# Streaming 32 columns in the narrow matmuls at the end of a cached-attention decode kernel, with a bias moved and two fills dropped

## The chip, the cores and the metric

The kernel runs on one NeuronCore of one Trainium2 chip. The metric is the device time of one execution, in microseconds (us). A profiled execution leaves a page and a trace; the span of a trace, from its first to its last instruction, is about 1.7 us shorter than the device time of the same execution. One execution of the kernel before, at 1652.69 us, was slow and is left out everywhere, from the medians too.

Names: PE is TensorE (its matmuls), PEld its weight loads, DVE is VectorE, ACT is ScalarE, SP is SyncE. L495 is line 495 of the kernel's file. Line numbers below L600 are almost the same in all versions; behind it they shift by a few lines, so each fence is introduced in words.

## The reference

One decode step for 8 sequences of one token: layer norm with modulation, grouped-query attention over a cache of 8192 positions (8 key/value heads, 32 query heads, 128 wide), the output projection, then a second layer norm and a two-layer MLP with squared ReLU.

```
h   = layernorm(x) * (1 + ca) + sa
q   = h @ wq                                   # 8 x 4096
p   = softmax(q k^T / sqrt(128))               # per head over 8192 positions
x   = x + ga * (concat(p v) @ wo)
h   = layernorm(x) * (1 + cb) + sb
x   = x + gb * (relu(h @ w1 + b1)**2 @ w2 + b2)
```

The caches are 268 MB in bf16, and they are read once.

## The kernel before

Keys and values come in tiles of 4 MB through a ring of four slots: for each of the 8 sequences four key tiles and four value tiles, each holding two heads. What matters here is the end: the value tiles of the last sequence, the output projection, the second norm and the MLP. `op` records an instruction for an engine with the tokens it waits for.

```python
def pe_stream(n, at):                       # "fills": results are never read
    rhs = IDENT[:, :].unsqueeze(1).to_broadcast([128, 4, 128])
    for _ in range(n):
        op("tensor", lambda e: e.matmul(bank(at)..., IDENT[:, :], rhs))          # 512 columns

wide = lambda ap, n=8: ap.unsqueeze(1).to_broadcast([128, n, B])                 # repeats the 8 columns n times
attn_w = bank(4)[:, 0:64 * KT].rearrange("p (k a b) -> p k a b", k=KT, a=8)

def project(q0, q1, k_oP):                  # output projection of the first heads, early
    ...
    op("tensor", lambda e: e.matmul(attn_w[:, k, :, :], wo_sb[...], wide(oP[:, j, g, :]), ...), [k_oP, d_woe])

# last sequence, value tiles p = 0, 1, 2
for m in range(32): ...                     # P @ V, 512 columns, four side by side in the array
t = op("vector", ... tensor_copy(osb, Obank))       # the copy: PE waits for it
...                                         # 4 small matmuls, a DVE multiply
if lastb and p == 1:
    k_oP = early(0, 2, ...)                 # 16 small matmuls and a DVE copy
    for f in range(FT): op("tensor", ... b1 into hT_ps ...)        # bias of the first MLP layer, 14 matmuls
    project(0, 2, k_oP)                     # first call, 64 matmuls
if lastb and p == 2:
    ...
    project(2, 3, k_oP)                     # second call, 32 matmuls

# last value tile (p = 3) arrives in four parts
for m in range(24):
    if m == 16:
        pe_stream(5, 7)
    ...                                     # parts 0 and 1
pe_stream(2, 7); direct(96, 112, ...)       # part 2, 32 columns
...; pe_stream(2, 7); direct(112, 128, ...) # part 3, 32 columns
...                                         # last projection, norm, first MLP layer (W1)
for f in range(FT):                         # second MLP layer (W2), 28 matmuls
    if f in (8, F2):
        pe_stream(1, 7)
    ...
```

The full listing follows.

## Time and profile before

| kernel before | value |
|---|---|
| time, the first three runs | 671.17 us median (671.04 to 671.33) |
| span of the trace | 669.8 us |
| DMA, HBM read | 423 GB/s, DMA busy nine tenths busy or more in all but the last slice |
| PE busy | 498.4 us (74%) |

The page's slices of the span (DMA busy in tenths), and its summary of the chain of work that ended last:

```profile
DMA  9999999999999999999999999999999999999996
PE 53%; DMA 37%; DVE 6%; ACT 2%; issue 1%; SPq 0%
```

Over most of the span DMA sets the pace. The next fence is the chain of waits of the kernel before in order of time: start, length, what. "PE PS L495 x64" is a run of 64 matmuls of line 495.

```profile
561.66 26.55 DMA ring<-in_A_k_cache_dram
...
644.88 3.25 PE PS L495 x64
648.13 2.13 PE PS L580 x32
...
652.25 1.15 PE PS L495 x32
653.40 0.98 PE PS L641 x16
654.38 1.19 PE PS L438 x5
655.57 0.55 PE PS L641 x8
...
658.05 0.20 DVE oTn L656
...
662.21 1.76 PE PS L699 x49
...
664.51 1.04 PE PS L716 x16
665.55 0.32 PE PS L438
665.88 0.53 PE PS L716 x8
666.41 0.32 PE PS L438
666.73 0.33 PE PS L716 x4
```

To be seen: after 588 us the chain never meets DMA again. L495 is the early projection (its first call takes 3.25 us, its second, half as many matmuls, 1.15 us), L580 the third value tile, L641 parts of the fourth, L438 the fills, L699 the first MLP layer, L716 the second with its two fills. A count can fall short of the matmuls issued, since the chain leaves some records out.

The trace also records when transfers land. The data are there before PE wants them (for parts 2 and 3 the first use is the weight load, elsewhere the first matmul):

```
                          landing us   first use by PE us
third value tile             646.5          648.06
fourth tile, part 0          651.4          653.3
fourth tile, part 1          653.9          655.5
fourth tile, part 2          655.2          656.3
fourth tile, part 3          656.5          657.2
W2, last part                665.3          666.66
```

So PE is about 0.75 us behind the last value part and 1.3 us behind the last weights. By this trace that is all there is to gain at this place.

The last view is the busy time of each engine in stretches of 3.41 us; the column after POOL is the granted TensorE clock as a share of full speed, then the DMA share and GB/s.

```profile
core 0: us, PE busy (x) PEld busy (x) DVE busy (x) ACT busy (x) POOL busy (x), PEclk, DMA share, GB/s
645.21:648.63 3.42, 3.42 (x65) 3.06 (x65) 0.00 (x0) 0.00 (x0) 0.00 (x0) 0.50 0.95 402
648.63:652.04 3.41, 2.32 (x54) 0.96 (x42) 0.95 (x3) 0.00 (x0) 0.00 (x0) 1.00 0.99 404
652.04:655.45 3.41, 3.23 (x55) 1.77 (x53) 0.15 (x1) 0.00 (x0) 0.00 (x0) 1.00 1.01 402
...
658.87:662.28 3.41, 2.75 (x34) 1.21 (x31) 1.65 (x9) 0.90 (x3) 0.00 (x0) 1.00 0.94 375
662.28:665.69 3.41, 3.07 (x73) 2.52 (x73) 0.78 (x4) 0.00 (x0) 0.00 (x0) 1.00 0.26 100
```

Each record of the clock but the last, which ends with the trace, lasts 3.413 us or a whole multiple of it (6.827, 20.48, 51.2), at 0.50 or 1.00; the stretches are cut at these borders. From 645.2 to 648.6 us PE had half its clock, and the early projection lies in just that stretch: its matmuls start 53 ns apart there, 31 ns apart in the second call. After 648.6 us the clock was full until the matmuls were over.

### The profile page before, as it was taken

To read this page: it belongs to the slowest core of one execution; us is meant where nothing else is said; L and a number is where in the kernel's file an instruction comes from. 1 tells how busy PE (TensorE), PEld (TensorE's weight loads), DVE (VectorE), ACT (ScalarE), POOL (GpSimd) and SP (SyncE) were. 2 spreads that over 40 slices of the span, in tenths; PEclk is the share of its full clock that TensorE was granted. 3 is DMA by queue.
4 is the path that set the end of the run, shared out by engine and by line. 5 is a ranking of instruction groups with operands and counts; after the bars stand their busy time and mean duration, and the time that the engine had idled before them with its cause. 6 is when DMAs were issued, how large, how long until landed. Compare 5 with 4: busy or idle time off the path is not lost.

```text
span 669.8 us, 16142 instructions
## 1 busy us (share of the span) xinstructions
PE 498.4 (74%) x7467; PEld 342.5 (51%) x7467; DVE 299.3 (45%) x568; ACT 235.1 (35%) x281; POOL 17.0 (3%) x67
## 2 busy tenths in 40 slices
PE   2295964799639993699648995399836996489977
PEld 2274731676218751477316762287415773177644
DVE  2153731466306661367315672166513673156722
ACT  2052620366105650266204660056402662046600
POOL 7200000000000000000000000000000000000000
PEclk9997996799958996699967998699966999579989
DMA  9999999999999999999999999999999999999996
GB/s 375 431 403 430 425 430 434 433 427 432 434 432 434 423 434 434 432 432 425 434 434 432 429 427 433 436 436 423 430 434 436 433 427 427 434 436 436 427 410 237
DMA packets 12970, 283.96 MB, mean 424 GB/s; under 512 B 1266, under 2 KB 2323, under 8 KB 4372
## 3 DMA queue, kind: packets, MB, share of 16 engines
q1 hardware_dynamic: 12900, 283.65, 98.9%
q8 instruction: 13, 0.21, 0.1%
q14 instruction: 9, 0.07, 0.0%
q10 hardware_dynamic: 48, 0.02, 0.0%
HBM read 283.66 MB, written 0.01 MB: 423 GB/s over the span
## 4 chain that ended last, share of the span: by engine, by line
PE 53%; DMA 37%; DVE 6%; ACT 2%; issue 1%; SPq 0%
DMA ring<-in_A_k_cache_dram 37%; PE PS L447 36%; PE PS L462 9%; DVE Pm L552 3%; PE PS L580 3%; ACT KTb L452 1%; PE PS L438 1%; ACT P_sb L530 1%; DVE m L467 1%; PE PS L539 1%; PE PS L495 1%; PE PS L559 0%; DVE O_sb L589 0%; DVE rhs_r L556 0%; DVE Dm L521 0%
## 5 line engine op out<-in xcount | busy, mean ns | idle before, releaser
L452 ACT ACTIVATE KTb<-PS 128x1024 bf16<-128x1024 bf16 x192 | 196.5, 1024 | 377.3 <-PE PS L447 377.3
L447 PE MATMUL PS<-IDENT,ring 128*128 128x128 bf16 x4096 | 267.4, 227 | 51.4 <-DMA ring<-in_A_k_cache_dram 42.7
L447 PEld LDWEIGHTS PS<-IDENT,ring 128*128 128x128 bf16 x4096 | 246.9, 102 | 99.7 <-DMA ring<-in_A_k_cache_dram 43.8
L454 DVE COPY KTb<-PS 128x1024 bf16<-128x1024 bf16 x320 | 209.8, 687 | 150.7 <-PE PS L447 148.5
L580 PE MATMUL PS<-ring,Pm 128*32 128x512 bf16 x992 | 81.4, 486 | 64.0 <-DMA ring<-in_A_v_cache_dram 63.1
L589 DVE CAST O_sb<-PS 128x512 bf16<-128x512 f32 x31 | 21.4, 691 | 145.0 <-PE PS L580 145.0
L462 PE MATMUL PS<-KTb,Qb 128*32 128x512 bf16 x1024 | 78.8, 384 | 4.5 <-ACT KTb L452 4.5
L580 PEld LDWEIGHTS PS<-ring,Pm 128*32 128x32 bf16 x992 | 29.1, 114 | 101.0 <-DMA ring<-in_A_v_cache_dram 64.4
L438 PE MATMUL PS<-IDENT 128*128 128x512 bf16 x137 | 36.3, 380 | 0.0
L593 PEld LDWEIGHTS PS<-SEL,O_sb 128*128 128x128 bf16 x124 | 5.3, 99 | 45.5 <-DVE O_sb L589 45.5
L530 ACT ACTIVATE P_sb<-PS,negm 128x512 bf16<-128x512 f32 x32 | 21.5, 685 | 18.9 <-DVE negm L526 18.9
L593 PE MATMUL PS<-SEL,O_sb 128*128 128x8 bf16 x124 | 8.0, 170 | 24.8 <-DVE O_sb L589 24.8
L462 PEld LDWEIGHTS PS<-KTb,Qb 128*32 128x32 bf16 x1024 | 15.4, 94 | 21.0 <-ACT KTb L452 8.5
L552 DVE COPY Pm<-PS 64x512 bf16<-64x512 bf16 x48 | 19.5, 419 | 13.4 <-PE PS L539 12.4
L467 DVE TENSOR_REDUCE m<-PS 128x1 f32<-128x512 f32 x32 | 22.0, 689 | 6.6 <-PE PS L462 6.6
L539 PE MATMUL PS<-IDENT,P_sb 128*64 128x128 bf16 x512 | 20.4, 222 | 2.0 <-ACT P_sb L530 1.2
L539 PEld LDWEIGHTS PS<-IDENT,P_sb 128*64 128x64 bf16 x512 | 15.2, 109 | 9.8 <-ACT P_sb L530 9.8
L438 PEld LDWEIGHTS PS<-IDENT 128*128 128x128 bf16 x137 | 11.3, 103 | 12.7 <-issue 4.7
L596 DVE TENSOR_TENSOR oTn<-PS,rinv 128x8 bf16<-128x8 f32 x31 | 6.0, 193 | 11.0 <-PE PS L593 11.0
L549 ACT ACTIVATE Pm<-PS 64x512 bf16<-64x512 bf16 x16 | 9.5, 592 | 1.1
L398 PE MATMUL PS<-haT,ring 128*128 128x8 bf16 x128 | 3.6, 168 | 7.5 <-DMA ring<-in_A_wq_dram 7.5
L689 ACT ACTIVATE std<-PS,epst 128x8 f32<-128x8 f32 x1 | 0.3, 267 | 23.3 <-PE PS L687 23.3
(114 smaller groups left out, 100.8 us busy)
## 6 DMA issues: line engine op xcount, KB each, us to landing
ring<-in_A_k_cache_dram SPq DMA_DIRECT2D x32, 4096.0 KB, 35.1
ring<-in_A_v_cache_dram SPq DMA_DIRECT2D x31, 4096.0 KB, 28.0
ring<-in_A_wq_dram SPq DMA_DIRECT2D x1, 4096.0 KB, 20.7
ring<-in_w_mod_dram SPq DMA_DIRECT2D x1, 3072.0 KB, 10.3
wo_sb<-in_A_wo_dram SPq DMA_DIRECT2D x1, 3072.0 KB, 45.6
ring<-in_A_v_cache_dram SPq DMA_DIRECT2D x1, 2048.0 KB, 22.5
ring<-in_B_w_dram SPq DMA_DIRECT2D x3, 512.0 KB, 17.6
ring<-in_B_w_dram SPq DMA_DIRECT2D x1, 1344.0 KB, 20.0
```

The costliest lines, as they stand in the source:

```text
L438: op("tensor", lambda e: e.matmul(bank(at).rearrange("p (a r) -> p a r", a=4), IDENT[:, :], rhs))
L447: t = op("tensor", lambda e, j=j, i=i: e.matmul(STG[j][:, i, :], src[:, 32 * k + 8 * j + i, :], IDENT[:, :], is_transpose=True), [loaded[n ...
L452: stg_free[j] = op("scalar", lambda e, j=j, dst=dst: e.activation(dst, STG[j], ACT.Copy), [t], "scaP")
L454: stg_free[j] = op("vector", lambda e, j=j, dst=dst: e.tensor_copy(dst, STG[j]), [t], "vecP")
L462: t = op("tensor", lambda e, hf=hf, q=q, rhs=rhs: e.matmul(PS[32 * q:32 * (q + 1), k, :], Qb[:, 2 * p + hf, :], rhs, start=(p == 0 and hf ...
L467: return op("vector", lambda e: e.tensor_reduce(m4[:, k:k + 1], bank(k), AX.X, ALU.max), [t])
L530: exps.append(op("scalar", lambda e, k=k: e.activation(P_sb[:, k, :], bank(k), ACT.Exp, bias=negm[:, 0:1], scale=inv_sqrt, accum_out=rs4[: ...
L539: t = op("tensor", lambda e, k=k, i=i, hf=hf, src=src: e.matmul(STG[k][64 * hf:64 * (hf + 1), i, :], src, IDENT[:, :], is_transpose=True, ...
L552: done.append(op("vector", lambda e, dst=dst, frm=frm: e.tensor_copy(dst, frm), [t, k_pm], "vecP"))
L580: t = op("tensor", lambda e, p=p, m=m, cg=cg, vt=vt, Obank=Obank: e.matmul(Obank[32 * cg:32 * (cg + 1), :], lhs[:, p, 32 * m:32 * m + 32], ...
L589: t = op("vector", lambda e, osb=osb, Obank=Obank: e.tensor_copy(osb, Obank), [t], "vecP")
L593: t = op("tensor", lambda e, i=i, osb=osb, oT_ps=oT_ps: e.matmul(oT_ps, osb[:, i * 128:(i + 1) * 128], SEL[:, i, :], start=(i == 0), stop= ...
```

## The change

The intent: make the early projection stream 32 columns instead of 64, since in the trace of before the 32-column matmuls of the fourth tile start 25 ns apart at full clock, and the 64-column ones of the projection 31 ns apart, 53 ns at half clock; put the bias matmuls where fills had been; drop the fills of the second MLP layer. The diff, with lines cut that only follow from it:

```diff
-        wide = lambda ap, n=8: ap.unsqueeze(1).to_broadcast([128, n, B])
-        attn_w = bank(4)[:, 0:64 * KT].rearrange("p (k a b) -> p k a b", k=KT, a=8)
+        wide = lambda ap: ap.unsqueeze(1).to_broadcast([128, 4, B])
+        attn_w = bank(4)[:, 0:32 * KT].rearrange("p (k a b) -> p k a b", k=KT, a=4)
...                                  (hT_w and oT_w likewise: PSUM spacing only)
                     if lastb and p == 1:
                         k_oP = early(0, 2, [norm_last, k_all] + stg_free + hold)
-                        for f in range(FT):
-                            op("tensor", ... b1 into hT_ps ...)
                         project(0, 2, k_oP)
...
                         if m == 16:
-                            pe_stream(5, 7)
+                            pe_stream(2, 7)
+                            for f in range(FT):
+                                op("tensor", ... b1 into hT_ps ...)
+                            pe_stream(2, 7)
...
         for f in range(FT):
-            if f in (8, F2):
-                pe_stream(1, 7)
```

The other narrow matmuls named in the change (fourth tile, first MLP layer) streamed 32 columns already.

More of the change, by code (lines that the diff above doesn't have):

```diff
@@ L471, in fcol @@
             return ap[:, 128 * a:128 * (a + j)].rearrange("o (p j) -> o j p", j=j)[:, f - a, :]
-        wide = lambda ap, n=8: ap.unsqueeze(1).to_broadcast([128, n, B])
-        attn_w = bank(4)[:, 0:64 * KT].rearrange("p (k a b) -> p k a b", k=KT, a=8)
+        wide = lambda ap: ap.unsqueeze(1).to_broadcast([128, 4, B])
+        attn_w = bank(4)[:, 0:32 * KT].rearrange("p (k a b) -> p k a b", k=KT, a=4)
         attn_ps = attn_w[:, :, 0, :]
-        hT_w = [bank(i)[:, 0:64 * 7].rearrange("p (f a b) -> p f a b", f=7, a=8) for i in range(2)]
+        hT_w = [bank(i)[:, 0:32 * 7].rearrange("p (f a b) -> p f a b", f=7, a=4) for i in range(2)]
         hT_ps = [h[:, :, 0, :] for h in hT_w]
@@ L600, in bass_adaLN_cond__gqa_block_cached__dense_activation_squared_relu__decode_kernel @@
                         k_oP = early(0, 2, [norm_last, k_all] + stg_free + hold)
-                        for f in range(FT):
-                            op("tensor", lambda e, f=f: e.matmul(
-                                hT_ps[f // 7][:, f % 7, :], fcol(b1_row[:], f), ONE8[:, :],
-                                start=(f % 7 == 0), stop=False, skip_group_check=True), [d_b2, s_bank_free[f // 7]])
                         project(0, 2, k_oP)
@@ L625, in bass_adaLN_cond__gqa_block_cached__dense_activation_squared_relu__decode_kernel @@
                             for i, (a, z, j) in enumerate(((0, 4, 4), (4, 8, 4), (8, 12, 4), (12, 14, 2)))]
-                    oT_w = bank(5)[:, 0:64].rearrange("p (a b) -> p a b", a=8)
+                    oT_w = bank(5)[:, 0:32].rearrange("p (a b) -> p a b", a=4)
                     oT_ps = oT_w[:, 0, :]
@@ L632, in direct @@
                             t = op("tensor", lambda e, m=m: e.matmul(
-                                oT_w[:, 0:4, :], vt[:, m, :], wide(lhs[:, NP - 1, 8 * m:8 * m + 8], 4), start=(first and m == a),
+                                oT_w, vt[:, m, :], wide(lhs[:, NP - 1, 8 * m:8 * m + 8]), start=(first and m == a),
                                 stop=(final and m == z - 1), skip_group_check=True), [loaded[n][i], k_rinv] + pmd[m // 32])
@@ L639, in bass_adaLN_cond__gqa_block_cached__dense_activation_squared_relu__decode_kernel @@
                         if m == 16:
-                            pe_stream(5, 7)
+                            pe_stream(2, 7)
+                            for f in range(FT):
+                                op("tensor", lambda e, f=f: e.matmul(
+                                    hT_ps[f // 7][:, f % 7, :], fcol(b1_row[:], f), ONE8[:, :],
+                                    start=(f % 7 == 0), stop=False, skip_group_check=True), [d_b2, s_bank_free[f // 7]])
+                            pe_stream(2, 7)
                         t = op("tensor", lambda e, m=m, cg=cg, vt=vt: e.matmul(
@@ L699, in bass_adaLN_cond__gqa_block_cached__dense_activation_squared_relu__decode_kernel @@
                     t = op("tensor", lambda e, f=f, k=k: e.matmul(
-                        hT_w[f // 7][:, f % 7, 0:4, :], wcol(k, f), wide(hbT[:, k, :], 4), start=False, stop=(k == KT - 1),
+                        hT_w[f // 7][:, f % 7, :, :], wcol(k, f), wide(hbT[:, k, :]), start=False, stop=(k == KT - 1),
                         skip_group_check=True), [k_hb, d_w1[k // (KT - 1)]])
```

## The prediction

Three passages are cut from the text, and the cuts are marked. None of them is a term of the sum: the 25 to 27 ns rest on the two spacings quoted right behind the first cut, and the sum comes to 0.6 us upstream and 0.64 us for the fills, about 1.25 us, as before.

> **What bounds the kernel.** DMA bounds the body: the page shows DMA at nine tenths or more in every slice but the last, 423 GB/s over the span. The chain of waits, though, leaves DMA at 588 us: from there to 668.0 us it is PE, with short DVE steps. The four parts of the last value tile land at 651.4, 653.9, 655.2 and 656.5 us; their first matmuls start at 653.3, 655.5, 656.3 and 657.2 (timeline). The last W2 part lands at 665.3; its matmuls start at 666.66. So at most about 1.3 us is to be had.
>
> **What changes.**
>
> 1. The early output projection streams 32 columns, not 64. In the timeline its first call (64 matmuls) takes 3.25 us, 644.8 to 648.1, because the granted clock is 0.50 from 645.2 to 648.6 us: there the starts lie 53 ns apart, elsewhere 31 ns. [...] here the 32-column value matmuls lie 25 ns apart at full clock, and the 8-column ones 27 ns at half clock. So I estimate 25 to 27 ns for 32 columns in both states: the first call takes about 1.7 us and ends near 646.5, exactly when the third value tile lands (646.5). That tile's matmuls start 1.5 us earlier, but 2.1 us of them instead of 0.5 us fall into the half-clock window, so they end only about 0.7 us earlier (estimate). The second call saves 32 x 6 ns = 0.2 us.
>
> 2. The bias matmuls (14 x 33 ns, 0.5 us) leave the place ahead of the first call. There they hid the DVE copy that the call needs (0.29 us): about 0.05 us is gained. In their new place they replace one of five fills (216 ns each): it costs 0.25 us.
>
> 3. The two fills of the second MLP layer go. Its matmuls resume 0.32 us after each: 0.64 us off the chain.
>
> 4. First MLP layer: only its PSUM spacing changes: nothing.
>
> Upstream gain: 0.05 + 0.65 + 0.2 - 0.25 = about 0.6 us at the last attention step. The last value part is then used at 656.6, 0.1 us after its landing. With the fills 1.25 us; the last four matmuls would start at about 665.4, at W2's landing.
>
> **Prediction.** 671.2 - 1.2 = 670.0 us, range 669.4 to 670.7. Far inside 2%: faster 0.01, same 0.98, slower 0.01.
>
> **What would show it right.** First projection call about 1.7 us with starts 27 ns apart at half clock; third value tile's matmuls from 646.5 us, partly at half clock, ending near 649.5; the matmuls of the last two value parts start about 0.6 us earlier; second MLP layer in one stretch of about 1.5 us (28 matmuls), whose last four wait little or not at all for W2. Landing times unchanged.
>
> **What would make it wrong.** The clock windows: fewer busy columns could bring one more half-clock window into 652 to 666 us, which costs up to 1 us or more; or in timed executions the window lies elsewhere, and the first call saves only 64 x 6 ns. [...] The last landings may vary by some tenths from run to run, and the new time would follow. [...]

## The result, and the profile after

| kernel | median us | lowest to highest | runs |
|---|---|---|---|
| before, beside it | 671.11 | 670.75 to 671.33 | 4 |
| changed | 672.29 | 672.16 to 673.29 | 4 |

The ratio is 1.0021 (95% interval 1.0004 to 1.0039). Ratios are the mean time of one kernel's runs over that of the other's of the same rounds, so not quite the ratio of the medians quoted. The changed kernel is slower by about 1.2 us, where a gain of 1.2 us was predicted. The trace of the changed kernel below is of the slowest of its four runs (673.29 us); the sums made from it hold for that execution.

The chain of waits of the changed kernel, the pieces that answer to those above (L642 are parts 0 and 1 of the fourth tile, L638 the moved bias, L700 and L715 the two MLP layers):

```profile
644.90 1.86 PE PS L495 x64
646.76 2.87 PE PS L580 x28
...
651.62 1.00 PE PS L495 x32
652.62 1.83 PE PS L642 x14
654.45 0.97 PE PS L438 x2
655.41 0.54 PE PS L638 x14
655.95 0.54 PE PS L438 x2
656.49 0.55 PE PS L642 x8
...
658.98 0.20 DVE oTn L657
...
663.13 1.79 PE PS L700 x49
...
665.47 3.17 PE PS L715 x28
```

To be seen: up to 652.6 us the change does what it should. The first projection call takes 1.86 us instead of 3.25, the third tile follows at once, and the fourth tile starts 0.78 us earlier than before (652.62 against 653.40). Then the lead is lost. The 16 matmuls of part 0 take 1.83 us where they took 0.98, the fills and the bias take 2.05 us (0.97, 0.54 and 0.54) where five fills took 1.19, and at the DVE multiply after the last value part (oTn) the kernel is 0.93 us late, which is just that sum: -0.78 + 0.85 + 0.86. The 28 matmuls of the second MLP layer take 3.17 us; before, with the two fills among them, they took 2.55.

The busy time and the clock of the changed kernel, in the stretches of its own clock records:

```profile
core 0: us, PE busy (x) PEld busy (x) DVE busy (x) ACT busy (x) POOL busy (x), PEclk, DMA share, GB/s
645.31:648.73 3.42, 3.42 (x75) 2.11 (x75) 0.00 (x0) 0.00 (x0) 0.00 (x0) 0.50 0.95 402
648.73:652.14 3.41, 2.14 (x59) 1.18 (x52) 1.11 (x3) 0.00 (x0) 0.00 (x0) 1.00 0.98 399
652.14:655.55 3.41, 3.41 (x42) 1.16 (x39) 0.00 (x0) 0.00 (x0) 0.00 (x0) 0.50 1.02 403
...
658.97:662.38 3.41, 2.88 (x48) 1.71 (x48) 1.26 (x7) 0.26 (x2) 0.00 (x0) 1.00 0.93 367
662.38:665.79 3.41, 2.92 (x62) 2.12 (x62) 1.36 (x7) 0.64 (x3) 0.00 (x0) 0.50 0.23 91
665.79:669.21 3.42, 2.84 (x28) 1.47 (x22) 0.51 (x3) 0.00 (x0) 0.00 (x0) 0.50 0.00 0
```

This is where the time went: three more stretches at half clock, one under the fourth tile and two under the MLP. DMA did not change: the last W2 part landed at 665.5 us (before 665.3).

### A number that the page does not have

PE busy does not say which stretch is followed by half clock: 2.88 us of 3.41 was (658.97), and 2.32 us was not (648.63, before). I therefore worked out from the traces an estimate, the share of each 3.41 us window in which columns stream: for each matmul its moving columns divided by a rate, from its start, overlaps counted once. The rate comes from two spacings in the trace of before: 512 columns of a fill in 216 ns at full clock are 2.37 per ns, and 128 columns of a transpose in 107 ns at half clock are 1.20, twice which is 2.4. Taken was 2.4 times the granted share; with 2.37 the counts of the traces of before and of the changed kernel stay the same. (The few fp32 matmuls were given a longer time, an assumption of mine that no trace shows; without it the counts below change by one or two.) Some matmul records can be missing, so the shares are good to some hundredths. All windows between 60 and 664 us of all 18 traces, by what the clock was in the window that followed:

```
window at full clock, streamed share    next: half   next: full
  under 0.34                                267            0
  0.34 to 0.38                                7           10
  0.38 to 0.42                                4           17
  over 0.42                                   0         2056
window at half clock, streamed share    next: half   next: full
  under 0.68                                492            0
  0.68 to 0.77                               34           21
  over 0.77                                   0          274
```

At half clock a share of 0.76 is as many columns as 0.38 at full clock. So in both parts of the table the outcome changes over at about the same number of columns. That is a count over these 18 traces and no more; what in the chip brings it about they do not show. Most of these windows lie in the body, which is the same in all kernels, and repeat each other; but of the 97 full-clock windows after 640 us, where the kernels differ, all 11 under 0.34 and none of the 66 over 0.42 were followed by half clock. In the kernel before, the window in which the third tile ends (648.63) had 0.49. In the changed kernel the same window (648.73) had 0.35: of the third tile's columns about 0.7 us fewer fall into it (0.9 us of its 2.87, against 1.6 us of 2.13), because the tile starts earlier and runs in the half-clock window before it.

Three more readings go with the count. Gaps of PE do not tell these windows apart: after 640 us, up to the last matmul, no gap of PE was longer than 0.80 us in the trace of before and 0.81 us in that of the changed kernel, and in the latter windows in which PE was busy for 63% (648.73) and 84% (658.97) were still followed by half clock. Transposes have to be counted: from 594 to 629 us (before) the clock is full while PE mostly transposes key tiles (32 transposes of 128 columns and, four side by side, 8 score matmuls of 512 in each 2.44 us); without the transposes the share there would be 0.17 (1024 columns of the 5856 that 2.44 us hold at 2.4 per ns), and all 267 windows under 0.34 lost the clock. And narrow matmuls add little to the share: 32 columns take 13 ns at that rate, of the 25 ns (full clock) or 27 ns (half clock) between two starts.

The half clock under the MLP is less plain. The window ahead of it (658.97) had 0.39, against 0.44 before (658.87): that lies in the strip where both outcomes were seen (0.34 to 0.42). Nothing in this window was narrowed; it holds other work because the kernel ran 0.93 us late. That the narrowing brought this loss too is argued, not shown.

The second fact is that the windows sat elsewhere from one traced execution to another. In the first two traces the half-clock window over the projection began at 645.2 and 645.3; window borders of later traces lie at 643.7, 644.1, 644.5, 645.7, 645.9, 646.5 and 646.9 us, spread over 3.2 us of a window's 3.41. So one trace shows one position of these borders (of "the grid"). That the times of one kernel scatter because of it is likely, but only the traces show the grid. The mean granted clock agrees loosely: slower runs tend to have the lower clock (correlation -0.45 over the 15 runs of the changed kernel, -0.46 over 50 of the kernel before).

### The profile page after: what moved, and what is told of

Read it like the earlier page. It is cut to its first block, busy times and chain, and to the rows that moved or that the text cites. A ratio compares the mean times of both kernels' runs of the same rounds, so it can differ in the third digit from the quotient of the medians.

```text
span 671.6 us, 16136 instructions
## 1 busy us (share of the span) xinstructions
PE 501.5 (75%) x7464; PEld 343.4 (51%) x7464; DVE 299.5 (45%) x568; ACT 235.1 (35%) x281; POOL 17.1 (3%) x67
## 4 chain that ended last, share of the span: by engine, by line
PE 53%; DMA 37%; DVE 6%; ACT 2%; issue 1%; SPq 0%
DMA ring<-in_A_k_cache_dram 37%; PE PS L447 36%; PE PS L462 9%; PE PS L580 3%; DVE Pm L552 3%; ACT KTb L452 1%; PE PS L438 1%; ACT P_sb L530 1%; DVE m L467 1%; PE PS L539 1%; PE PS L559 0%; PE PS L715 0%; PE PS L495 0%; PE PS L642 0%; DVE O_sb L589 0%
## 5 line engine op out<-in xcount | busy, mean ns | idle before, releaser
L452 ACT ACTIVATE KTb<-PS 128x1024 bf16<-128x1024 bf16 x192 | 196.5, 1024 | 377.4 <-PE PS L447 377.4
```

The source lines that it names most:

```text
L452: stg_free[j] = op("scalar", lambda e, j=j, dst=dst: e.activation(dst, STG[j], ACT.Copy), [t], "scaP")
```

## The experiments

"A" is the theory that fewer streamed columns bring additional half-clock windows. Its rivals: B, the dropped fills or the moved bias did it; C, a fixed cost in the changed code; D, it is issue activity and not columns that holds the clock; E, with the clock up, narrower matmuls do gain what they save in spacing. All kernels gave correct results. Of the ratios to the kernel before, only those of the first result, e9 and e13 (slower) and of e8 and e16 (faster) have a 95% interval that leaves out 1; the other differences of medians are not clear of noise one by one.

### One part at a time

**e1_cols_only.** The projection alone at 32 columns, all else as before.

```diff
-   attn_w[:, k, :, :], wo_sb[...], wide(oP[:, j, g, :])
+   attn_w[:, k, 0:4, :], wo_sb[...], wide(oP[:, j, g, :], 4)
```

> The kernel before with the early projection alone at 32 columns. Theory A (the narrower projection moves the third value tile's matmuls into the half-clock window, so that too few columns stream between about 648.7 and 652.1 us, and the clock is halved again from 652.1 to 655.5): the projection takes about 1.8 us, the share of the 648.7 window in which columns stream is about 0.35 (before 0.49), half clock from about 652.1 to 655.5, time 671.5 to 672.5. Rival B (the missing fills of the second MLP layer or the moved bias brought the half clock): full clock from 648.7 on and about 670.3.

Measured: 671.30 us median (671.22 to 672.81; before beside it 671.05), in two groups: three runs at 671.2 to 671.3, two at 672.6 and 672.8. Its trace, busy time and clock:

```profile
core 0: us, PE busy (x) PEld busy (x) DVE busy (x) ACT busy (x) POOL busy (x), PEclk, DMA share, GB/s
647.49:650.90 3.41, 2.15 (x55) 1.11 (x48) 1.11 (x3) 0.00 (x0) 0.00 (x0) 1.00 0.94 388
650.90:654.31 3.41, 3.41 (x45) 1.40 (x42) 0.00 (x0) 0.00 (x0) 0.00 (x0) 0.50 1.01 405
```

The window after the third tile (share 0.38) is followed by half clock although the projection itself had run at full clock in this execution. The narrow projection alone does not gain; B falls for this part. The time was below A's range in three of the five runs. The trace is of one of these three, and it lost a window too; why the other two runs are 1.3 us slower was not seen. In this execution the projection ended before the third tile had landed (646.60): PE waited 0.56 us for it, so the first call had nothing to gain.

**e2_bias_only.** Bias moved alone.

```diff
@@ before project(0, 2, k_oP)
-   for f in range(FT): op("tensor", ... b1 ...)
@@ fourth tile, m == 16
-   pe_stream(5, 7)
+   pe_stream(2, 7); for f in range(FT): op("tensor", ... b1 ...); pe_stream(2, 7)
```

> The kernel before with the bias matmuls moved alone. Theory A: projection as slow as before (3.25 us), no further half-clock window after 648.6, about 0.2 us lost in the new place: 671.2 to 671.5. Rival B (moved bias is the cause): a half-clock window after 648.6 and 672 or more.

Measured: 670.97 us median (670.69 to 671.77), before 671.05; 671.2 to 671.5 had been expected under A. The move alone costs nothing that can be told from the scatter. Its trace did show half-clock windows after 648.6 (650.9 to 654.3 and 661.2 to 664.6), which the expectation excluded: so a kernel with the wide projection can get them too.

**e3_nofill_only.** No fills in the second MLP layer, all else as before.

```diff
-   if f in (8, F2):
-       pe_stream(1, 7)
```

> The kernel before without the two fills of the second MLP layer alone. Theory A: full clock to the end, second MLP layer in about 1.55 us instead of 2.55 us less 0.3, time 0.5 to 0.65 us less: 670.4 to 670.7. Rival B (the fills hold the clock up): half clock before 667 us and no gain, 671 or more.

Measured: 670.55 us median (670.31 to 670.76), before 671.05, as A expected (ratio 0.9991, interval 0.9977 to 1.0004). In its trace the 28 matmuls take 1.71 us and the clock is full from 648 us to the last matmul. The clock stayed up in this execution without the fills; rival B falls here too.

**e4_after_wide.** The changed kernel with the projection back at 64 columns.

```diff
-   wide = lambda ap: ap.unsqueeze(1).to_broadcast([128, 4, B])
-   attn_w = bank(4)[:, 0:32 * KT].rearrange("p (k a b) -> p k a b", k=KT, a=4)
+   wide = lambda ap, n=4: ap.unsqueeze(1).to_broadcast([128, n, B])
+   attn_w = bank(4)[:, 0:64 * KT].rearrange("p (k a b) -> p k a b", k=KT, a=8)
...
-   wo_sb[...], wide(oP[:, j, g, :])
+   wo_sb[...], wide(oP[:, j, g, :], 8)
```

> The changed kernel with the early projection put back to 64 columns; bias moved and no fills as in the change. Theory A: both further half-clock windows vanish (full clock from 648.7 to the end of the matmuls), time 670.6 to 671.0, faster than before and 1.3 to 1.7 us faster than the changed kernel. Rival B: half clock stays at 652 or 662 us and the time stays at about 672.

Measured: 670.46 us median (670.18 to 671.38), before 671.05. That is about 1.8 us under the first four runs of the changed kernel, and 0.6 us under the kernel before beside it (interval 0.9978 to 1.0005). Two windows of its trace:

```profile
core 0: us, PE busy (x) PEld busy (x) DVE busy (x) ACT busy (x) POOL busy (x), PEclk, DMA share, GB/s
645.65:649.07 3.42, 1.91 (x32) 0.77 (x32) 0.55 (x1) 0.00 (x0) 0.00 (x0) 1.00 0.98 407
655.89:659.31 3.42, 2.65 (x61) 1.67 (x59) 0.73 (x4) 0.00 (x0) 0.00 (x0) 1.00 1.04 408
659.31:662.72 3.41, 3.41 (x42) 2.00 (x41) 1.12 (x7) 0.90 (x3) 0.00 (x0) 0.50 0.86 341
```

The expected full clock "to the end" was wrong, and usefully so. The window at 645.65 is PE-busy for 56% (share 0.51) and keeps the clock; the one at 655.89 is PE-busy for 78%, with 32- and 8-column matmuls (share 0.29), and loses it. Busy time does not tell these two apart.

**e9_cols_bias** and **e10_cols_nofill.** The two remaining combinations: narrow projection with the bias moved, and narrow projection without the fills, by the same edits as above.

> Narrow projection and moved bias, with the two fills of the second MLP layer kept. Theory A: the half-clock window after the third tile comes in most executions as with the whole change; the fills cost about 0.6 us more: median 672.2 to 673.2. Rival B (missing fills of the second MLP layer are what makes the change slow): 671 or less.

> Narrow projection and no fills in the second MLP layer, with the bias in its old place, where it hides the copy. Theory A: as with the narrow projection alone (671.3 and 672.7) less the 0.6 us of the fills: 670.6 to 672.1, median about 670.8, so the moved bias (one fill less ahead of the fourth tile, 0.25 us longer chain, an idle 0.45 us ahead of the projection) adds to the loss only together with the narrow projection. Rival B: as slow as the whole change, 672.2.

Measured: e9 672.23 us median (671.53 to 674.29); e10 672.11 us median, two runs at 670.7 and 670.8, three at 672.1 to 672.3 (before beside both 671.09). e9 came out as A expected and rules out B's 671 or less: with the fills kept, the time was still up. The median expected for e10 was missed, and 672.11 is close to the number put down for B; by itself e10 does not tell the two apart. Its two groups are those of e1 less about 0.5 us. All combinations:

| narrow projection | bias moved | no fills | median us | runs |
|---|---|---|---|---|
| no | no | no | 671.09 | 54 |
| no | yes | no | 670.97 | 5 |
| no | no | yes | 670.55 | 5 |
| no | yes | yes | 670.46 | 5 |
| yes | no | no | 671.30 | 5 |
| yes | yes | no | 672.23 | 6 |
| yes | no | yes | 672.11 | 5 |
| yes | yes | yes | 672.20 | 15 |

The lower half of the table is the upper one with the narrow projection: it is slower with it in each pair, by 0.2 to 1.7 us (second median less first: 671.30 - 671.09, 672.20 - 670.46). Dropping the fills alone gives a median 0.5 us lower. With five runs that fall into groups a single median is rough.

### The changed kernel again

**e5_after_again** and, later, **e15_after_third**: the changed kernel without any edit.

> The changed kernel itself once more, five rounds and a second trace. Theory A as refined (the clock is granted in windows of 3.41 us whose position against the kernel differs from execution to execution; a window at full clock in which columns stream for less than about 0.39 of the time is followed by one at half clock, 8 of 8 last windows of the traces so far within 0.02 of that): the window grid lies elsewhere than in the first trace, the times scatter over 1 us or more, 670.8 to 673.3, median about 672. Rival C (a fixed cost in the changed code, the same in each execution): all times within 0.4 us and the same half-clock windows as in the first trace.

> The changed kernel a third time, beside the other two on the same chip. Theory A: most runs between 671.9 and 673.3, perhaps one near 670.6 where the windows lie well.

Measured: e5 672.19 us median (670.63 to 673.02, before 671.19); e15 671.88 (670.85 to 672.81, before 670.94; two of its five runs lie in the range that most were expected in). With the first four runs these are 15: median 672.20, 670.63 to 673.29. The kernel before has 54 timed runs: median 671.09, 670.62 to 672.83. The traces of e5 and e15 have their half-clock windows at 646.5 to 650.0 and 653.4 to 656.8, and at 645.9 to 656.1 and 662.9 to 666.3. So the windows move, the times scatter over 2.7 us, and rival C falls: the best run of the changed kernel equals the best of the kernel before.

### Giving the clock its columns back

**e6_after_fill3.** While PE waits 0.7 us for the copy of the third tile, it streams three fills. At full clock they take 0.65 us (3 x 216 ns), less than the 0.70 us of the copy; at half clock they took 1.40 us (see e14).

```diff
     t = op("vector", ... tensor_copy(osb, Obank))
+    if lastb and p in (2,):
+        Pg.wait("tensor", stg_free + hold)
+        pe_stream(3, 7)
```

> The changed kernel with three fills (0.65 us of streamed columns) added while TensorE waits 0.7 us for the copy of the third tile's result; they delay nothing. Theory A: the share of streamed columns in the window that follows the third tile rises by about 0.19 to over 0.5, no half clock between about 651 and 656 us, median 0.8 to 1.8 us below the changed kernel, 670.3 to 671.3. Rival C: same time as the changed kernel, or later by the fills.

Measured: 670.36 us median (670.24 to 671.14), before 671.19. Its trace:

```profile
core 0: us, PE busy (x) PEld busy (x) DVE busy (x) ACT busy (x) POOL busy (x), PEclk, DMA share, GB/s
644.70:648.11 3.41, 3.27 (x80) 2.21 (x80) 0.00 (x0) 0.00 (x0) 0.00 (x0) 0.50 0.98 418
648.11:651.53 3.42, 2.91 (x57) 1.28 (x50) 1.11 (x3) 0.00 (x0) 0.00 (x0) 1.00 0.95 390
651.53:654.94 3.41, 3.41 (x65) 1.76 (x65) 0.00 (x0) 0.00 (x0) 0.00 (x0) 1.00 1.02 407
```

The half clock over the projection is there as before, but the window after the third tile now has a share of 0.57, and the fourth tile runs at full clock.

**e14_after_fill3_again.** The same kernel once more, later.

> The changed kernel with three fills of 512 columns in the copy of the third tile, once more, beside the other two on the same chip. Theory A: all runs at 670.2 to 671.2. If two or more of five are at 671.9 or more, the earlier result was luck with the position of the windows.

Measured: 671.26 us median (670.18 to 672.98), before 670.94; one run of six over 671.9, two more over 671.5. That is worse than expected. The trace of its slowest run shows why: the window at 642.6, ahead of the projection, has a share of 0.29, and the clock stays halved from 646.0 to 656.2, because at half clock even the filled window reaches 0.74, in the strip (0.68 to 0.77) after which the clock stayed at half 34 times of 55. The fills cost time there as well: at half clock they last 1.40 us, twice the copy, and the matmul that needs the copy starts 0.45 us after its end (651.66 against 651.21), against 0.05 us in e15 without them. Of the 11 runs of the two calls one is over 671.9, against 10 of 15 of the changed kernel. Three fills help; they were not enough for the position of the windows in this trace.

**e7_after_fill123.** Three fills in the copies of the first, second and third tile (`p in (0, 1, 2)`).

> As the run before it, with three fills in the copies of the first and second tile too. Theory A: the half-clock window at about 645 us goes as well, the projection takes about 1.7 us at 25 ns in every execution; at the end the last weights bound it, so little more is gained: 670.1 to 671.0. Rival C: no gain.

Measured: 670.39 us median (670.27 to 671.1), before 671.19. As expected but for the one run at 671.1, 0.1 us over; in its trace the clock is full from 592.5 to 667.6 us.

**e12_wide_fill123.** The same fills, with the projection at 64 columns.

> Projection at 64 columns, bias moved, no fills in the second MLP layer, three fills in each of the three copies. Theory A: with the clock kept up the 64 columns cost 64 x 6 ns more in the first call, hidden behind the landing of the third tile, so the last weights bound it too: 670.2 to 670.6 with a scatter under 0.5 us, equal to the narrow projection with the same fills; narrowing then gains nothing. Rival E (narrowing gains what its 6 ns for each matmul say): 0.5 us slower than the narrow one with fills.

Measured: 670.41 us median (670.22 to 670.91), before 671.09; one run is outside the expected 670.2 to 670.6. Equal to the narrow one with the same fills (e7). So the columns that the change saves are worth nothing here once the clock is up (670.41 against 670.39 us); rival E falls. Its trace shows why: at full clock the 64-column projection too is done before the third tile lands (646.33; its matmuls start at 646.37).

**e8_full_clock** and, later, **e16_full_clock_again.** Narrow early projection, bias in its old place where it covers a DVE copy, fills in all three copies, no fills in the second MLP layer, and the last projection widened from 8 to 32 columns.

```diff
+    if lastb and p in (0, 1, 2):
+        Pg.wait("tensor", stg_free + hold)
+        pe_stream(3, 7)
...
-    pe_stream(2, 7); <bias>; pe_stream(2, 7)          # and <bias> back ahead of project(0, 2)
+    pe_stream(2, 7); pe_stream(3, 7)
...
-    attn_ps[:, k, :], wo_sb[:, 24 + x, ...], oTn[...]
+    attn_w[:, k, :, :], wo_sb[:, 24 + x, ...], wide(oTn[...])
```

> Narrow early projection, bias in its old place (it hides the copy), no fills in the second MLP layer, three fills in each of the three copies, and the last projection widened from 8 to 32 columns, which its 25 ns spacing should hide. Theory A: no half-clock window from 640 us to the last matmul in any position of the grid; the last weight part (landing at about 665.3) bounds the end: 670.1 to 670.5 with a scatter under 0.4 us, faster than before by 0.6 to 1.0 us. Rival C: no better than without the additions.

> The version with fills in all three copies, the narrow early projection, the widened last projection, the bias in its old place and no fills in the second MLP layer, once more, because a repeat of another version showed how small samples mislead. Theory A: no full-clock window after 640 us has a streamed share under 0.42, wherever the grid lies, so all runs stay within 670.2 to 670.9; if one is at 671.5 or more, it is not robust.

Measured: 670.40 us median (670.29 to 670.47, before 671.19, ratio 0.9985, interval 0.9972 to 0.9998), and 670.39 (670.24 to 670.45, before 671.43, ratio 0.9984, interval 0.9970 to 0.9998). Ten runs within 0.23 us, all under the best of the kernel before (670.62). The end of the chain of waits of e8 (L718 is its second MLP layer):

```profile
649.63 15.10 DMA ring<-in_B_w_dram
664.73 0.04 issue
664.77 0.60 PE PS L718 x8
665.38 0.03 issue
665.40 0.40 PE PS L718 x4
```

The chain now ends with the arrival of W2: the last four matmuls start at 665.40, its last part landed at 665.36. This is the bound that the prediction named. The expectation of e16 was missed in one point: its trace has a full-clock window with a share of 0.36 (643.5) and a half-clock window from 646.9 to 650.3. Its time, 670.30 us, was no worse for it: the second MLP layer still ended at 665.80 us, as in e8 (665.80). So the scatter is small although a window can still be halved; that the windows are rarer and that there is slack behind them is the likely reason.

### Columns or activity

**e11_after_narrow_fill** and **e13_after_onecol_fill.** In the copy of the third tile, 26 matmuls of 8 columns, or of one column, in place of e6's three fills. They keep PE issuing for about the same 0.65 us.

```diff
+    if lastb and p in (2,):
+        Pg.wait("tensor", stg_free + hold)
+        for _ in range(26):
+            op("tensor", lambda e: e.matmul(bank(7)[:, 0:8], IDENT[:, :], IDENT[:, 0:8]))   # e13: 0:1
```

> The changed kernel with 26 matmuls of 8 columns (0.65 us at 25 ns) in the copy of the third tile, where an earlier run had three fills of 512 columns. Theory A (what keeps the clock is streamed columns; these are 208 columns against 1536): share of streamed columns in the following window still under about 0.38, the clock is halved as in the changed kernel, median about 672, scatter over 1 us. Rival D (any issue activity that closes the idle gap keeps the clock): no half clock from 650 to 656 us, about 670.4.

> The changed kernel with 26 matmuls of a single column in the copy of the third tile: the engine issues and loads weights for about 0.65 us as with the 8-column ones, but streams 26 columns (0.01 us) in place of 208. Theory A (streamed columns keep the clock): like the changed kernel, most runs at 671.9 or more and a half-clock window that begins between 651 and 655 us in most traces. Rival D (closing the issue gap keeps it): like the three wide fills, all runs under 671.2.

Measured: e11 670.64 us median, four runs at 670.3 to 670.9 and two at 672.5, and a share of 0.42 in its trace: 208 columns brought it to the upper end of the strip in which both outcomes were seen, so the trace told nothing apart. The expectation under A was missed, and the four runs are what D had put down. e13: 672.05 us median (670.62 to 673.33, before 670.94). Its trace shows that the single-column matmuls do fill the gap:

```profile
L595 PE MATMUL PS<-IDENT x26: 163/163/177, 648.7 to 649.3; 128*128 128x1 bf16 x26
```

Closing the gap without columns gained nothing in these six runs, though their range overlaps that of e14. The one trace of e13 happens to be of its fastest run, in a position where no window before the last matmuls falls under 0.38, so the half-clock window that I expected "in most traces" was not shown by it. That D falls rests more on the traces: on the windows of e4, where 78% busy lost the clock and 56% kept it, and on a count over the 97 full-clock windows after 640 us. If each matmul is counted as at least 25 ns, the spacing of the 8-column matmuls at full clock, so that issue activity counts in place of columns, shares from 0.43 to 0.66 occur with both outcomes, and 54 of the windows lie there; by PE busy time it is 0.56 to 0.84, with 47. By streamed columns it is 0.38 to 0.40, with 13.

## Why the prediction was wrong

1. **What bounds the kernel: right.** PE's chain after 588 us, and the last weights at 665.3 behind it. e8 and e16 reach that bound at 670.4 us.
2. **Step 1, the narrow projection, taken by itself: right for this position of the clock windows.** The first call took 1.86 us (1.7 predicted) with starts 27 ns apart at half clock; the third tile ran from 646.7, mostly at half clock, and ended at 649.6 (649.5 predicted); the second call took 1.00 us instead of 1.15. The fourth tile began 0.78 us earlier.
3. **Step 2, the moved bias: put too low.** 0.25 us was put down for its new place. Where the clock was full (e4, e6, e7, e12), fills and bias took 1.60 to 1.62 us there, against 1.19 for the five fills of before: about 0.42 us more. The time of e2, 0.08 us less than before, is nothing within the scatter.
4. **Step 3, the fills: right within the noise.** 0.64 us predicted; alone it measured 0.50 (e3), and in the changed kernel's trace, at half clock, it was swallowed.
5. **The step that failed** is the sum "Upstream gain: 0.05 + 0.65 + 0.2 - 0.25 = about 0.6 us". It carried over the clock of the one trace of before, half from 645.2 to 648.6 and full from there on, into a kernel that streams fewer columns, and so it counted every matmul of the fourth tile at full clock; the runs showed half clock there. The missing term in the first trace is 1.46 us under the fourth tile: part 0 took 0.85 us longer and fills with bias 0.86 us longer, less the 0.25 that had been put down for the bias. Of this, 0.17 us is the bias term that was too low at any clock. A second missing term is 1.46 us in the second MLP layer, which took 3.17 us at half clock against 1.71 at full clock in e3 and e5.
6. **The risk was named and put too low.** "Fewer busy columns could bring one more half-clock window into 652 to 666 us" is just what happened, in the first trace with three. The prediction put it at up to 1 us or more and listed it as a reserve, with no share of streamed columns worked out, though the trace of before had over a hundred windows from which the share that loses the clock could have been read: of its full-clock windows from 60 to 664 us the 13 up to 0.37 were followed by half clock, the 115 from 0.38 up were not. The prediction even had the number: 2.1 us instead of 0.5 us of the third tile in the half-clock window are 0.8 us of full-rate columns taken from the next one (1.6 us at half rate), 0.23 of a window. That takes 0.49 to 0.26; the second call, which moves into the window, gives back some, and the trace shows 0.35.
7. **A position was taken for a property.** In the traces the window borders lie anywhere between 643.7 and 646.9 us. The prediction named another position among its risks ("the first call saves only 64 x 6 ns"), and still reckoned with the one of its trace. At another position even this saving was not to be had: with the projection at full clock PE waits for the third tile, 0.56 us in e1 and 1.46 us in e15, and the earlier end of the first call only adds to the wait.

What stays open: how much of the loss each window position brings, since only the traces show the windows; and whether what counts is exactly the streamed columns or something that goes with them. The count as made here separates all but 38 of 2361 full-clock windows cleanly.

## What to carry to other kernels

Before making matmuls narrower, or moving work off PE's idle stretches, work out for each 3.4 us how many columns still stream. In these traces all 267 full-clock windows with a share under 0.34 were followed by half clock and none of the 2056 over 0.42, and a saving reckoned at half a microsecond cost one and a half (0.65 us against 1.46 us, fourth tile). Where PE waited for another engine anyway, wide fills that fit the wait (three of 216 ns in a copy of 0.70 us) cost nothing that could be measured at full clock, and with them in all three copies the clock stayed full from 592.5 to 667.6 us (e7); at half clock the same fills outlasted the wait (0.4 us in e14), and without the fills on the chain the median was 0.5 us lower (e3). Take several traces before reckoning with a clock window, because its position changed from run to run (by up to 3.2 us here), and judge such changes by the spread as well as by the median.
